# Landing tiles, residual rows and the order of W's transfers in the 16-point stage of a spectral kernel

## The chip, the cores and the metric

The kernel runs on one core of one Trainium2 chip. The metric is the device time of one execution in microseconds (us). Engines: TensorE (PE) multiplies, VectorE (DVE) and ScalarE (ACT) work element by element, GpSimd (POOL) and SyncE (SP) mostly issue transfers (DMAs). Each engine works its own instruction queue in order, and so does SP with the DMAs that it issues.

## What is computed

Four layers in turn on x of 2048 rows and 576 columns: a Fourier mixing layer A, a long-convolution layer B, and both again with the same matrices.

```python
def A(x):                     # y = Re(C (x W)), C: 2048 x 2048, W: 576 x 576
    a, b = x @ W_re.T, x @ W_im.T
    return C_re @ a - C_im @ b

def B(q, k, v, shift_k, ssm_k, ssm_D):
    kv = shift_conv4(k, shift_k) * v
    y = irfft(rfft(pad(kv)) * rfft(pad(ssm_k)))[:2048] + kv * ssm_D
    return q * y              # q: the normed rows

x = x + A(norm(x)); x = x + B(norm(x), K, V, ...)
x = x + A(norm(x)); x = x + B(norm(x), K, V, ...)
```

The convolution's result does not depend on x (only the gate q does), so it is computed once, beside the first layer A, and used by both layers B.

## The kernel before, in words

**Layer A.** C (`c_mat`) is walked in steps of one 128x512 piece: `layer` (L297) loops over four blocks of output rows (tb), two parts (g: real, imaginary) and 16 pieces (k). That is 128 steps for the first layer A, 32 to a block. A step has 14 matmuls of 512 columns: 12 into four accumulators `s`, 2 into `rm` for the last 64 columns of x (the remainder rows). `load_c` (L214) keeps two pieces in flight: it loads a piece into a raw tile (ring `craw`) by a DMA on SP, and splits it into a rounded high part (ACT, L93) and a low part (DVE, L94) in tiles `cs` (three of them, in `mats`). Each such load is kept behind the one before it, and `load_after` (L165) keeps other loads behind the newest of them. At the end of a g (steps 15, 31, 47, 63 and so on) the accumulators are split into `u`, and `evac_r` (L263) brings the remainder rows through a scratch tile (ring `rt`, words RT_AT on of the big tile `flts`): ACT copy L269, DVE add L270, then a split (ACT L93, DVE L94, written `u<-flts`).

**Hidden rows.** When a block is done, its four groups of 128 rows are multiplied by W in `hidden` (L273): a residual row x is loaded (SP, L276), and for each half of 288 columns 27 matmuls go into one PSUM tile `bk`, which DVE adds to the residual (L284); then the row is stored (`done0`, SP, L686) into `xa`. There are three `bk` tiles, shared with the convolution. Two residual tiles of 576 words (ring `res`) are in turn. At the end of the first g of the next block (steps 47, 79, 111) PE works through those of the four rows that are left.

**W.** `load_w` (L226) brings W in nine pieces through a ring of three raw tiles `wl` (DMAs on SP: L233, the last piece L235 and L236), and ACT and DVE split each (L93 and L94, from the fifth on L105 and L106). It runs from step 41 to 45.

**The convolution** is a generator, `branch` (L344), of which the main loop takes a piece now and then. Its first part (to step 42) ends in stores `t<-flts` from a ring of four tiles `so`. Its second part, the 16-point stage, begins at step 45 (`MID_LOAD`) and is spread from step 47 to 111 by planned costs. It works a list `feeds` of 96 items: 64 "mid" items (16-point transforms and the product with the kernel, 9 matmuls of 288 columns: `mid_kernel`, `mid_signal`, `mid_inverse`), whose results go to `v_d` (`vd<-flts`, ACT queue), and 32 rows of the inverse (`i2_products`, 12 matmuls), which read `v_d`. Ten of the 16 inverse rows of the first half stand between the mid items of the second half, every second one from item `I2_FIRST` on; the others come after the last mid item. Each item's input, a feed, is loaded into a landing tile (ring `land`, two of 576 words; `flts<-t` for a mid item, `flts<-vd` for an inverse row, both issued from SP at L167), then split by `act_split` (ACT L509 for the first and L507 after that, DVE L513) two items ahead of its use. After item i the feed i+4 is asked for, into the tile from which feed i+2 has just been split. All ACT work of this stage is kept in the order of the program (L504 to L509).

**The order of the work** on each engine's queue is made when the program is built: a planner goes by program order, dependences (overlapping words of a tile are one) and a model of costs, and may bring an instruction forward that has nothing to wait for. `behind(...)` and `issue_after` keep an instruction behind a named one on the same engine.

**The words of `flts`** in the 16-point stage: two raw tiles `craw` (512 words) in 88 to 1111; `res` 1112 to 2263; `land` 2264 to 3415; `kk` 3416 to 4567; four `vo` tiles of 288 from 4568 to 5719; `rt` 5464 to 5975. Before that stage `so` lay in 1112 to 3415 and the W tiles `wl` lie in 3416 to 5143.

Of the kernel before, what the change touches and what calls it, by code (L numbers as in the profile page):

```python
# [13 lines left out]
OP = mybir.AluOpType  # L14

P = 128
S = 2048
D = 576
J = S // P
TB = 4  # L20
NT = 512
HD = D // 2
NC = 4
REM = D - NC * P
# [15 lines left out]
I2_END = 111  # L40
PREP = 113
MID_LAG = 2
BORDER = {J - 1: 0.5, 0: 0.75}
I2_FIRST = 37
I2_LATE = 6
I2_COST = 2.0
GROUPS = 2
# [6 lines left out]
CRAW = 2  # L54
# [6 lines left out]
SC_AT = 8 + 4 * STAT  # L61
RT_AT = SC_AT + 4 * REM + 5 * WIDE
# [4 lines left out]
def fnet_h3_kernel(ctx: ExitStack, tc: tile.TileContext, x, c_mat, w_re, w_im, k_pad, v, shift_k,  # L67
                   ssm_k, ssm_d, f1c, i2c, midc, out):
    nc = tc.nc
# [26 lines left out]
    @contextmanager  # L96
    def behind(*instructions):
        with ExitStack() as stack:
            for i in instructions:
                stack.enter_context(tc.issue_after(i))  # L100
            yield
# [27 lines left out]
    ring = {}  # L129

    def lay(t, at, *sizes):

        for name, words, n in sizes:
            ring.setdefault(name, Ring()).tiles.extend(t[:, at + i * words:at + (i + 1) * words] for i in range(n))
            at += n * words
        assert at <= t.shape[1], (at, t.shape, sizes)
        return at
# [18 lines left out]
    flts = flat(FLT, F32, "flts")  # L156
# [6 lines left out]
    anchor, made, rounded, pows, biased, halved, added, evac, parted, stored = [], [], [], [], [], [], [], [], [], []  # L163

    def load_after(dst, src):  # L165
        with tc.issue_after(anchor[-1]):
            return nc.sync.dma_start(dst, src).ins  # L167
# [37 lines left out]
    xa_d = [dr.tile([P, D], F32, name=f"xa{j}") for j in range(J)]  # L205
# [15 lines left out]
            halved[:] = split(t[0], t[1], raw)  # L221
        CT[step] = t

    W = []

    def load_w():  # L226
        lay(flts, SC_AT + CRAW * NT + 4 * D, ("wl", D, 3))
        wg = region_a(FR, "w").rearrange("p (k n) -> p k n", k=9)
        for ch in range(9):
            w = two(wg[:, ch])  # L230
            raw = ring["wl"]()
            if ch < 8:
                nc.sync.dma_start(raw, (w_re if ch < 4 else w_im)[(ch % 4) * P:(ch % 4 + 1) * P, :])  # L233
            else:
                nc.sync.dma_start(raw[:REM], w_re[NC * P:, :])  # L235
                nc.sync.dma_start(raw[REM:], w_im[NC * P:, :])  # L236
            if ch < 4:
                split(w[:, 0, :], w[:, 1, :], raw)
            else:
                signed_split(w[:, 0, :], w[:, 1, :], raw, -1.0 if ch < 8 else mixed)  # L240
            W.append(w)
            yield
        for ch in range(9):
            load_after(w_d[ch], wg[:, ch].bitcast(F32))
            yield
# [26 lines left out]

    def hidden(us, tb, jj, xres, done, late=False):  # L273
        j = TB * tb + jj
        r = ring["res"]()
        (load_after if late else nc.sync.dma_start)(r, xres(j))  # L276
        for hf in range(2):
            ps = bank()
            cs = slice(hf * HD, (hf + 1) * HD)
            for ch in range(9):  # L280
                for n, (a, b) in enumerate(((0, 0), (0, 1), (1, 0))):
                    mm(ps[:, :HD], us[ch][:, a, jj * P:(jj + 1) * P], W[ch][:, b, cs],
                       ch == 0 and n == 0, ch == 8 and n == 2)
            added[:] = [nc.vector.tensor_tensor(r[:, cs], r[:, cs], ps[:, :HD], OP.add).ins]  # L284
            yield
        done(j, r)

    def finish(pending, pieces):
        while pending and pieces:
# [54 lines left out]
    def branch():  # L344
# [131 lines left out]
        for left_over in split_up:  # L476
            yield from f1_products(*left_over)
        m1 = region_b(FR, "mid")
        kk_at = SC_AT + CRAW * NT + 4 * D
        at = lay(m1, 0, ("df", 2 * D, 3), ("mc", 4 * P, 1))  # L480
        fresh("land", "fc")
        old = ring["craw"]
        held = [t for t in (old() for _ in range(3)) if t is not old.tiles[CRAW]]
        fresh("craw")
        ring["craw"].tiles.extend(held)
        spare = at
        at = lay(m1, at, ("yf", D, 2))
        lay(m1, at, ("fc", 4 * P, 2))
        at = lay(flts, SC_AT + CRAW * NT, ("res", D, 2))
        lay(flts, at, ("land", D, 2), ("kk", D, 2), ("vo", HD, 4))  # L490
        mc = quads(ring["mc"]())
        load_fr(mc, midc)
        lo, hi = slice(0, 64), slice(64, 128)
# [74 lines left out]
        def load_feed(i):  # L568
            if i < len(feeds):
                kind, hf, q = feeds[i]  # L570
                landed[i] = ring["land"]()
                load_after(landed[i], v_d[hf][:, q].rearrange("p c d -> p (c d)") if kind else
                           t_d[hf][4 * q:4 * q + 4].rearrange("q j c s d -> (q j c) (s d)"))
# [8 lines left out]
                halves[i] = parts("df")  # L582
                act_split(*halves[i], landed.pop(i))

        load_feed(0)
        load_feed(1)
        yield 0
        for i in range(2):
            split_feed(i)
            load_feed(i + 2)  # L590
            load_fc(i)
        used, ahead, product = 0, 2, None
        for i, (kind, hf, q) in enumerate(feeds):
            df = halves.pop(i)
            if kind:
                i2_products(hf, q, fcs.pop(used), df)
                load_fc(used + ahead)
                used += 1
            else:
                if len(yfs) == MID_LAG:  # L600
                    mid_inverse(*yfs.pop(0))
                    yield 0.4
                kk = mid_kernel(df)
                if product is not None:
                    yfs.append((*product[:2], mid_round(product[2])))
                yield 1.6
                product = hf, q, mid_signal(df, kk)
            split_feed(i + 2)
            load_feed(i + ahead + 2)
            if i == last_mid:  # L610
                yield 0.4
                mid_inverse(*yfs.pop(0))
                yfs.append((*product[:2], mid_round(product[2])))
                while yfs:
                    yield 0.4
                    mid_inverse(*yfs.pop(0))
                for name, t, at, words in (("fc", m1, spare, 4 * P), ("land", flts, kk_at, D)):
                    old = ring[name]
                    held = [old.tiles[(old.n + m) % 2] for m in range(2)]
                    fresh(name)  # L620
                    lay(t, at, (name, words, 2))
                    ring[name].tiles.extend(held)
                for m in range(2):
                    load_fc(used + ahead + m)
                    load_feed(i + ahead + 3 + m)
                ahead = 4
            yield I2_COST if kind else 1.1

# [53 lines left out]
            next(ln, 0)  # L682
            X[j] = to_x(src, j)

    def done0(j, xa):
        nc.sync.dma_start(xa_d[j], xa)  # L686

    def make_x1(j):
        xa, q = ring["xa"](), ring["yb"]()
# [63 lines left out]
    for n, whole in layer(get_x0, lambda j: x[:, j, :], done0, pending):  # L753
        if (whole or whole is not None and n % J < J - 1) and n <= F1_END:
            at = n if whole else n - 0.5
            at16 = 4 + 2 * F1_16
            want = int(4 + F1_16 * at / 8 if at <= 16 else at16 + (68 - at16) * (at - 16) / (F1_END - 16))
            with behind(made[min(n + 2, J - 1)], *evac):
                while used < want:
                    next(br)  # L760
                    used += 1
        if whole is not None and n >= W_FROM and len(W) < 9:
            with behind(*stored):
                next(wl)
        if whole and n == MID_LOAD:
            next(br)
        if n >= MID_FROM:
            if whole is not None:
                passed += STEP * (4 if whole else 3) / 7 * BORDER.get(n % J, 1.05)
            if whole is None or whole and n % 2 == 1 and n % (2 * J) < J - 1 and pending:  # L770
                finish(pending, 1)
                passed += PIECE
            near = whole and n % J == J - 2 or whole is False and n % J == J - 1
            for _ in range(0 if near else GROUPS):
                if spent < work * min(1.0, passed / total):
                    with behind(*added, *evac):
                        spent += next(br, work)
        if not whole:
            continue
        if n >= W_SAVE and n % 2 == 0:  # L780
            next(wl, 0)
        m = n - PREP
        if m == 0:
            lay(flts, SC_AT + CRAW * NT + 2 * D, ("xa", D, 2), ("yb", D, 2))
            old = ring["craw"]
            held = [old(), old()]
            fresh("craw")
            lay(flts, SC_AT + CRAW * NT + 6 * D, ("craw", NT, 1))
            ring["craw"].tiles.extend(held)
            gate = region_b(F32, "gate")  # L790
            lay(gate, 0, ("xa", D, 4), ("yb", D, 4), ("xj", D, 2))
        if 0 <= m and n < HOLD:
            advance(m // 2 if m % 2 == 0 and m < 2 * EARLY else None)
# [328 lines left out]
```

## Time and profile before

| | |
|---|---|
| runs shown | 1197.28, 1197.49, 1197.61 us; median 1197.49 |
| profiled execution | 1196.82 us, of which the span from first to last instruction is 1195.0 |
| granted clock of PE | 0.999 |
| PE busy | 1175.8 us |
| DVE, ACT, POOL busy | 839.1, 637.5, 74.0 us |
| DMA queue of SP | 205.58 MB |

How to read the profile's lines: `L76 PE MATMUL bk<-mid 128x288 ... x627 | 106.9, 299 | 2.9 <-ACT ...` is a group of instructions of line 76 that write `bk` and read `mid`: how many, busy us in total, mean ns of one, and the idle time of the engine just before them with what ended it. In a list of waits, "SPq L167 <- DVE mid L513: total, times, longest" says that the DMA issued at line 167 waited for DVE's instruction of line 513. In a timeline a row has start and duration in us; what stands in brackets is the idle time before it and who ended it. Durations of matmuls overlap, so their mean is longer than the distance from one to the next.

### The profile page before, as it was taken

Reading aid. Unit: us, or ns where it says so; the run is one execution under the profiler, and the core shown is the slowest. Engines: PE = TensorE matmul, PEld = TensorE weight load, DVE = VectorE, ACT = ScalarE, POOL = GpSimd, SP = SyncE. Lnnn points to the kernel's source line nnn. Section 1 sums busy time; section 2 is a strip of 40 time slices with the busy share of each in tenths; the row PEclk is TensorE's granted clock in tenths of the full one; section 3 lists DMA queues with packets and bytes.
Section 4 is the critical chain, followed back from the end, with each engine's and each line's share of the span. In section 5 each row is a group of like instructions: output and inputs, shape, how many; then the busy total and the mean of one; then the engine's idle time right before and its main releaser. Section 6 shows DMA issues by size and latency. Waiting matters only on the chain.

```text
span 1195.0 us, 18251 instructions
## 1 busy us (share of the span) xinstructions
PE 1175.8 (98%) x6320; PEld 1028.1 (86%) x6320; DVE 839.1 (70%) x1495; ACT 637.5 (53%) x1266; POOL 74.0 (6%) x116
## 2 busy tenths in 40 slices
PE   7999999999999999999999999999999999999997
PEld 6888888988888888889988898888888888889997
DVE  7899794679877677675447766774775776874764
ACT  7965655477766567665435666544434435540200
POOL 2200000000000000001101121000000000001111
PEclk9999999999999999999999999999999999999999
DMA  9889898546756657658967686872592597696621
GB/s 355 279 268 308 258 300 279 154 136 192 210 190 191 216 165 220 200 143 240 317 198 242 221 255 215 272 266 71 168 313 93 163 317 273 201 350 190 219 83 41
DMA packets 146110, 261.96 MB, mean 219 GB/s; under 512 B 15841, under 2 KB 44769, under 8 KB 146018
## 3 DMA queue, kind: packets, MB, share of 16 engines
q1 hardware_dynamic: 102674, 205.58, 54.1%
q10 hardware_dynamic: 36432, 42.63, 10.2%
q0 software_dynamic: 6912, 12.59, 4.0%
q8 instruction: 50, 0.82, 0.3%
q14 instruction: 42, 0.34, 0.1%
HBM read 194.09 MB, written 66.65 MB: 218 GB/s over the span
## 4 chain that ended last, share of the span: by engine, by line
PE 74%; ACT 3%; DVE 3%; issue 1%; DMA 1%; ACTq 0%; POOLq 0%; DVEq 0%
PE s L76 41%; PE bk L76 29%; PE rm L76 4%; ACT flts L507 2%; DVE mid L513 1%; ACT mid L507 1%; DMA flts<-t 1%; DVE u L94 0%; DVE flts L527 0%; DMA flts<-vd 0%; ACT u L93 0%; DVE flts L526 0%; DVE flts L528 0%; ACT mats L93 0%; DVE flts L270 0%
## 5 line engine op out<-in xcount | busy, mean ns | idle before, releaser
L76 PE MATMUL s<-mats 128*128 128x512 f32 x2088 | 528.2, 392 | 0.3 <-DVE u L94 0.2
L76 PEld LDWEIGHTS s<-mats 128*128 128x128 f32 x2088 | 381.5, 188 | 69.2 <-DVE u L94 0.6
L93 ACT ACTIVATE mats<-flts 128x512 fp32r<-128x512 f32 x201 | 125.8, 627 | 91.5 <-PE rm L76 33.4
L94 DVE TENSOR_TENSOR mats<-flts,mats 128x512 fp32r<-128x512 f32 x201 | 137.3, 687 | 51.6 <-ACT mats L93 50.4
L507 ACT ACTIVATE flts<-bk 64x288 f32<-64x288 f32 (+1 forms) x288 | 115.7, 406 | 105.0 <-PE bk L76 83.0
L513 DVE TENSOR_TENSOR mid<-flts,mid 128x576 fp32r<-128x576 f32 (+1 forms) x160 | 102.0, 638 | 45.6 <-ACT mid L507 38.0
L76 PE MATMUL bk<-mid 128*128 128x288 f32 x768 | 128.5, 298 | 2.9 <-ACT flts L507 1.8
L76 PEld LDWEIGHTS bk<-mid 128*128 128x128 f32 x768 | 114.8, 188 | 19.1 <-ACT flts L507 7.7
L76 PE MATMUL bk<-w,u 128*128 128x288 f32 x864 | 120.5, 295 | 1.5 <-DVE flts L284 1.0
L76 PEld LDWEIGHTS bk<-w,u 128*128 128x128 f32 x864 | 117.4, 188 | 4.8 <-DVE flts L284 1.7
L76 PE MATMUL rm<-mats 128*128 128x512 f32 x304 | 94.4, 390 | 0.0
L507 ACT ACTIVATE mid<-flts 128x576 fp32r<-128x576 f32 (+1 forms) x159 | 87.0, 581 | 12.0 <-DMA flts<-vd 6.7
L443 ACT ACTIVATE flts<-bk 128x288 f32<-128x288 f32 x128 | 50.7, 409 | 48.1 <-PE bk L76 47.5
L76 PEld LDWEIGHTS bk<-f1r 128*128 128x128 f32 x384 | 59.8, 192 | 13.2 <-ACT f1r L93 6.4
L76 PE MATMUL bk<-f1r 128*128 128x288 f32 x384 | 64.6, 301 | 6.7 <-ACT f1r L93 6.4
L76 PE MATMUL bk<-mats 128*128 128x288 f32 (+1 forms) x376 | 67.9, 317 | 0.0
L284 DVE TENSOR_TENSOR flts<-flts,bk 128x288 f32<-128x288 f32 x48 | 21.8, 453 | 65.0 <-PE bk L76 64.9
L76 PEld LDWEIGHTS rm<-mats 128*128 128x128 f32 x304 | 56.9, 188 | 11.8
L76 PE MATMUL s<-t,mats 128*128 128x512 f32 x264 | 64.9, 389 | 0.0
L185 POOL TENSOR_TENSOR flts<-flts 128x1 f32<-128x1 f32 x35 | 29.6, 844 | 522.7 <-DVE flts L184 522.7
L76 PE MATMUL bk<-mats,t 128*128 128x288 f32 (+1 forms) x368 | 59.3, 303 | 0.0
L76 PEld LDWEIGHTS bk<-mats 128*128 128x128 f32 x376 | 55.6, 188 | 3.4
(148 smaller groups left out, 1434.2 us busy)
## 6 DMA issues: line engine op xcount, KB each, us to landing
flts<-in_c_mat SPq DMA_DIRECT2D x148, 256.0 KB, 3.7
ph<-in_c_mat SPq DMA_DIRECT2D x54, 512.0 KB, 4.5
t<-flts ACTq DMA_DIRECT2D x64, 288.0 KB, 4.9
flts<-t SPq DMA_DIRECT2D x64, 288.0 KB, 3.1
flts<-in_c_mat SPq DMA_DIRECT2D x30, 512.0 KB, 5.1
vd<-flts ACTq DMA_DIRECT2D x64, 144.0 KB, 2.9
flts<-vd SPq DMA_DIRECT2D x32, 288.0 KB, 4.5
mid<-in_i2c POOLq DMA_DIRECT2D x32, 256.0 KB, 5.1
```

What stands on the lines that cost most here:

```text
L76: nc.tensor.matmul(ps, lhsT, rhs, start=first, stop=last, skip_group_check=more)
L93: a = nc.scalar.activation(h, src, AF.Copy).ins
L94: return a, nc.vector.tensor_tensor(l, src, h.bitcast(F32), OP.subtract).ins
L185: pows.append(nc.gpsimd.tensor_tensor(rs, ve, mhalf, OP.pow).ins)
L284: added[:] = [nc.vector.tensor_tensor(r[:, cs], r[:, cs], ps[:, :HD], OP.add).ins]
L443: stored[:] = [nc.scalar.activation(so[:, c, :], ps[:, :HD], AF.Copy).ins]
L507: last_act.append(nc.scalar.activation(*args, **kw).ins)
L513: nc.vector.tensor_tensor(l, src, h.bitcast(F32), OP.subtract)
```

## The change

Five edits, with new places for tiles:

1. `LANDS = 3`: three landing tiles (2552 to 4279); after item i the feed i+5 is asked for (later i+7 where it was i+6), and three feeds are asked for at the start.
2. `I2_FIRST` goes from 37 to 38: the first late row, and the nine that follow, stand one item later.
3. In the first layer A a residual row is loaded as two halves by two DMAs into a ring of three tiles of 288 words (1112 to 1975), and each half is stored by a DMA of its own once the next piece is taken. The late rows of the second layer stay whole.
4. The residual rows' loads, and the start of the 16-point stage, are kept behind the last DMA of W on SP.
5. Places in the stage: the two raw tiles of `c_mat` lie at 8 to 519 and at RT_AT (5464 to 5975, the place of `rt`); `vo` at 520 to 1095 and 1976 to 2551; `kk` 4280 to 5431. At step 113 three raw tiles are laid anew.

```diff
+LANDS = 3
-I2_FIRST = 37
+I2_FIRST = 38
@@ load_w
-                nc.sync.dma_start(raw[REM:], w_im[NC * P:, :])
+                asked[:] = [nc.sync.dma_start(raw[REM:], w_im[NC * P:, :]).ins]
@@ hidden
-        r = ring["res"]()
-        (load_after if late else nc.sync.dma_start)(r, xres(j))
+        if late:
+            r = ring["res"]()
+            load_after(r, xres(j))
+            rows = [r[:, :HD], r[:, HD:]]
+        else:
+            rows = [ring["res"]() for _ in range(2)]
+            with behind(*asked):
+                for hf in range(2):
+                    nc.sync.dma_start(rows[hf], xres(j)[:, hf * HD:(hf + 1) * HD])
...
-            added[:] = [nc.vector.tensor_tensor(r[:, cs], r[:, cs], ps[:, :HD], OP.add).ins]
+            added[:] = [nc.vector.tensor_tensor(rows[hf], rows[hf], ps[:, :HD], OP.add).ins]
             yield
-        done(j, r)
+            if not late:
+                done(j, cs, rows[hf])
+        if late:
+            done(j, r)
@@ branch
-        kk_at = SC_AT + CRAW * NT + 4 * D
+        kk_at = 1976 + 2 * HD + LANDS * D
...
-        old = ring["craw"]
-        held = [t for t in (old() for _ in range(3)) if t is not old.tiles[CRAW]]
         fresh("craw")
-        ring["craw"].tiles.extend(held)
...
-        at = lay(flts, SC_AT + CRAW * NT, ("res", D, 2))
-        lay(flts, at, ("land", D, 2), ("kk", D, 2), ("vo", HD, 4))
+        lay(flts, lay(flts, 8, ("craw", NT, 1)), ("vo", HD, 2))
+        lay(flts, RT_AT, ("craw", NT, 1))
+        at = lay(flts, SC_AT + CRAW * NT, ("res", HD, 3), ("vo", HD, 2), ("land", D, LANDS))
+        assert at == kk_at
+        assert lay(flts, at, ("kk", D, 2)) <= RT_AT
...
-        load_feed(0)
-        load_feed(1)
+        for i in range(LANDS):
+            load_feed(i)
         yield 0
         for i in range(2):
             split_feed(i)
-            load_feed(i + 2)
+            load_feed(i + LANDS)
             load_fc(i)
...
             split_feed(i + 2)
-            load_feed(i + ahead + 2)
+            load_feed(i + ahead + LANDS)
...
-                    held = [old.tiles[(old.n + m) % 2] for m in range(2)]
+                    held = [old.tiles[(old.n + m) % len(old.tiles)] for m in range(len(old.tiles))]
...
-                    load_feed(i + ahead + 3 + m)
+                    load_feed(i + ahead + LANDS + 1 + m)
@@ done0
-    def done0(j, xa):
-        nc.sync.dma_start(xa_d[j], xa)
+    def done0(j, cs, xa):
+        nc.sync.dma_start(xa_d[j][:, cs], xa)
@@ main loop of the first layer
         if whole and n == MID_LOAD:
-            next(br)
+            with behind(*asked):
+                next(br)
...
         if m == 0:
...
-            old = ring["craw"]
-            held = [old(), old()]
             fresh("craw")
             lay(flts, SC_AT + CRAW * NT + 6 * D, ("craw", NT, 1))
-            ring["craw"].tiles.extend(held)
+            lay(flts, SC_AT, ("craw", NT, CRAW))
```

More of the change, by code (lines that the diff above doesn't have):

```diff
@@ L222, in load_c @@
         CT[step] = t
-    W = []
+    W, asked = [], []
     def load_w():
```

## The prediction

> **What bounds the kernel now.** I read the head of the page first, then busy time by stretches, then the groups of TensorE (PE) instructions in the stretch that the change touches, then the waits, and last the chain of waits.
>
> ```profile
> span 1195.0 us, 18251 instructions
> PE 1175.8 (98%) x6320; PEld 1028.1 (86%) x6320; DVE 839.1 (70%) x1495; ACT 637.5 (53%) x1266; POOL 74.0 (6%) x116
> ```
>
> PE is the bound, and the change removes no matmul. All that it can win is time in which PE is held up, and only between about 200 us (W arrives) and 550 us (the last 16-point item). A row of busy time by stretches has for each engine the busy us and the instructions in brackets.
>
> ```profile
> 200.00:550.00 350.00, 345.35 (x1960) 303.25 (x1959) 261.02 (x503) 229.33 (x493) 6.50 (x13) 1.00 0.62 187
> 200.00:225.00 25.00, 23.72 (x136) 20.67 (x135) 13.96 (x24) 12.12 (x23) 1.21 (x3) 1.00 0.74 222
> 440.00:460.00 20.00, 18.83 (x101) 15.39 (x100) 18.28 (x36) 16.10 (x36) 1.05 (x2) 1.00 0.69 201
> 1076.00:1176.00 100.00, 100.00 (x757) 100.00 (x756) 61.27 (x130) 11.58 (x18) 14.10 (x14) 1.00 0.45 148
> ```
>
> PE is idle 350 - 345.35 = 4.65 us there. Matmuls overlap, so idle time understates the loss; the pace is the better measure. Undisturbed pace of 512-column matmuls, from the timeline of PE (start, us, what): 12 + 2 of them between 625.81 and 628.99, 3.18 / 14 = 0.227 us each. Of 288-column ones, which alone run at the end: 100 / 757 = 0.132 us.
>
> ```profile
> 625.81 2.88 PE L76 MATMUL s<-mats 128*128 128x512 f32 x12
> 628.53 0.62 PE L76 MATMUL rm<-mats 128*128 128x512 f32 x2
> 628.99 2.88 PE L76 MATMUL s<-mats 128*128 128x512 f32 x12
> ```
>
> The groups of PE in 200 to 550:
>
> ```profile
> L76 PE MATMUL s<-mats 128*128 128x512 f32 x706 | 183.3, 392 | 0.2 <-DVE u L94 0.2
> L76 PE MATMUL bk<-mid 128*128 128x288 f32 x627 | 106.9, 299 | 2.9 <-ACT flts L507 1.8 <-DVE flts L527 0.3
> L76 PE MATMUL bk<-w,u 128*128 128x288 f32 x509 | 71.3, 296 | 1.5 <-DVE flts L284 1.0 <-DVE w L106 0.3 <-ACT flts L507 0.2
> L76 PE MATMUL rm<-mats 128*128 128x512 f32 x118 | 36.5, 390 | 0.0
> ```
>
> 824 x 0.227 + 1136 x 0.132 = 187.0 + 150.0 = 337.0 us; 350 - 337.0 = **13 us is all there is to win**, 1.1% of the kernel. The Trainium skill (Perfetto Trace Analysis, Identifying the Most-Contended Engine) would judge the headroom by the busy share of weight loads; here that is 303.25 of 350, which would leave 47 us, but the same share is 86% over the whole kernel, where most stretches lose nothing, so the pace decides.
>
> **The change part by part.** *(a) W ahead of the residual rows.* SyncE (SP) works its queue in order. Four of its rows, from its timeline:
>
> ```profile
> 201.95 0.33 SPq L276 DMA_DIRECT2D flts<-in_x  x1
> 204.24 0.33 SPq L167 DMA_DIRECT2D flts<-t  x1
> 204.69 0.42 SPq L233 DMA_DIRECT2D flts<-in_w_im  x1
> 208.67 0.34 SPq L167 DMA_DIRECT2D flts<-t  x1
> ```
>
> A residual row (201.95) and the first feed of the 16-point stage (204.24) stand ahead of a W piece (204.69), which so goes at least 204.69 - 201.95 = 2.7 us later than SP came to the first of them. PE pays when the first hidden row reaches the last W pieces (waits of PE in 205 to 225: total, times, longest):
>
> ```profile
> PE bk L76 <- DVE flts L284: 1.0, 2, 0.7
> PE bk L76 <- DVE w L106: 0.3, 1, 0.3
> ```
>
> The 0.3 is W's own split; the 1.0 is the add of the first half row, late because VectorE (DVE) works W's and c_mat's splits ahead of it. Earlier W pieces clear both: -1.3, bounds 0 and -1.3. Against it stands the first feed: the new landing tiles (words 2552 to 4279) lie on the last two store tiles of the stage before and on W's raw tiles, so the first feed can no longer go at 204.24 but about where the second goes now, 208.67. The second's split on ScalarE (ACT) was
>
> ```profile
> 215.15 0.67 ACT L507 ACTIVATE mid<-flts 128x576 fp32r<-128x576 f32 x1
> 216.00 0.43 PE L76 MATMUL bk<-mid 128*128 128x288 f32 x2
> ```
>
> and PE's first 16-point matmul began at 216.00. A first feed that is split at 215.15 is ready at 215.82 on ACT and some 0.7 later on DVE: +0 to +0.6. I take +0.3. Sum of (a): **-1.0**, bounds -1.3 and +0.6.
>
> *(b) Third landing tile.* With two tiles, feed i+4 goes where feed i+2 lay; with three, feed i+5 does. Both wait for the same split, at the same place in the program: SP's wait stays, but the data has one item more before it is needed. The place where that matters is 440 to 460, where late rows (feeds from vd) lie between the 16-point feeds (from t). The chain of waits there, and ACT at its end:
>
> ```profile
> 442.42 2.85 DMA flts<-vd
> 451.97 3.49 DMA flts<-t
> 454.74 0.68 ACT L507 ACTIVATE mid<-flts 128x576 fp32r<-128x576 f32 x1 [1.36 <-DMA flts<-vd]
> ```
>
> 6.3 of these 20 us of the chain are transfers into landing tiles. PE's groups in 440 to 460:
>
> ```profile
> L76 PE MATMUL s<-mats 128*128 128x512 f32 x42 | 12.4, 393 | 0.0
> L76 PE MATMUL bk<-mid 128*128 128x288 f32 x51 | 9.7, 304 | 1.2 <-ACT flts L507 1.0
> L76 PE MATMUL rm<-mats 128*128 128x512 f32 x8 | 2.5, 393 | 0.0
> ```
>
> 50 x 0.227 + 51 x 0.132 = 18.1 of 20 us: **1.9 us lost**. I take all of it as won: the late DMA comes first in that chain. If ACT (16.10 busy of 20) and DVE (18.28) are late next, it is 0. The other bound is all the time that ACT waits for feeds in 200 to 550:
>
> ```profile
> ACT mid L507 <- DMA flts<-vd: 4.4, 5, 1.4
> ACT mid L507 <- DMA flts<-t: 1.7, 2, 1.3
> ```
>
> 4.4 + 1.7 = 6.1. So (b): **-1.9**, bounds -6.1 and 0. The late rows one item later (I2_FIRST) cancel the longer lead for these rows: the first late feed is asked for after the same item as before, so it waits no longer for the store of the half that it reads. Cost 0. After the last 16-point item the lead is seven feeds, not six; PE waits for nothing from 550 to 630 beyond what (b) covers. Cost 0.
>
> *(c) Residual rows in halves.* 16 rows of one load and one store become 32 of each, so 32 more issues of 0.33 us on SP, 11 us in some 400 in which SP mostly waits. What counts is what SP waits for at them (waits of SP in 224 to 630):
>
> ```profile
> SPq L167 <- DVE mid L513: 175.6, 86, 5.5
> SPq L276 <- DMA xa<-flts: 25.2, 10, 5.2
> SPq L686 <- DVE flts L284: 18.6, 10, 5.3
> ```
>
> A load of a row waits for the store of an older row to land (2.5 us), a store for its add (1.9 us); behind them stand feeds and c_mat loads. Halves double these waits and shift the stores forward by half a row. While SP waits there, the feed behind it would mostly wait for its split (2.0 us each) anyway: cost 0; without that cover, as much as (b) wins, +1.9, since it is the feeds that come late. The Trainium skill (DMA: Bandwidth & Descriptors, Rules for kernel authors) speaks against this part: many small transfers are to be put together, since a fixed part dominates. The trace agrees on the fixed part:
>
> ```profile
> flts<-t SPq DMA_DIRECT2D x64, 288.0 KB, 3.1
> vd<-flts ACTq DMA_DIRECT2D x64, 144.0 KB, 2.9
> ```
>
> Half the bytes take 2.9 instead of 3.1 us to land, so two halves in a row would take 2.7 us more for each row. This falls on PE only if something waits for it; a half row is needed some 3.5 us after its matmuls begin (27 x 0.132), as now.
>
> *(d) c_mat's raw tiles.* One of the two now lies where the remainder rows' scratch tile (rt) lies. At each block end (steps 47, 63, 79, 95, 111) the load of c_mat four steps on has to wait until that tile's last reader, DVE's split, is done, where it now goes ahead. Step 79 from the timelines of SP, DVE and ACT, and the issue row of c_mat:
>
> ```profile
> 428.60 0.33 SPq L167 DMA_DIRECT2D flts<-in_c_mat  x1
> 440.08 0.69 DVE L94 TENSOR_TENSOR u<-flts,u 64x512 fp32r<-64x512 f32 x1
> 441.82 0.63 ACT L93 ACTIVATE mats<-flts 128x512 fp32r<-128x512 f32 x1
> flts<-in_c_mat SPq DMA_DIRECT2D x148, 256.0 KB, 3.7
> ```
>
> The load moves from 428.60 to 440.77, lands at 440.8 + 3.7 = 444.5, and its split, now at 441.82, moves 2.7 us back. PE needs that matrix only at step 83, three steps after the end of step 79; 50 matmuls of 512 in 20 us are 3.6 steps of 14, so a step takes 5.6 us here and 16 us remain. The shortest time is after step 111, where a step takes 3.18 us and step 115 begins at 628.99 (above):
>
> ```profile
> 621.84 0.68 DVE L94 TENSOR_TENSOR u<-flts,u 64x512 fp32r<-64x512 f32 x1
> ```
>
> 622.5 + 3.7 + 1.3 for the split = 627.5, 1.5 us to spare. So cost 0 if ACT does other work meanwhile; up to +2.7 at each of the four ends inside the stage if ACT stands at that split with 16-point work queued behind it: +10.8.
>
> **Sum:** -1.0 - 1.9 + 0 + 0 = -2.9 us on the profiled execution (1196.82 us: the span of 1195.0 and 1.8 around it). The median of the runs shown is 1197.49, 0.7 above it; the forecast is 1197.5 - 2.9 = **1194.6 us**, by itself 1192.5 to 1196. About 0.2% (2.4 us) is what a measurement of this kernel tells from no change, so the forecast lies close to that edge.
>
> **The rivals.**
>
> *Hidden, or taken back.* PE's stalls between 250 and 440 come from ACT and DVE in turn, not from transfers (of PE's idle time before 16-point matmuls, 1.8 of 2.9 us ends with ACT's copy L507). Where the feed comes earlier, the same chain is late next; or the half rows delay the feeds on SP by as much as the third tile gives them. For it: DVE's 18.28 of 20 us. Against it: ACT does wait for the feed at 454.74. Then only (a) is left, or less: 1197.5 - 0.5 = **1197.0**.
>
> *More freedom.* The feed one item earlier lets ACT and DVE run ahead throughout: all 6.1 us of (b) and 1.0 of (a): **1190.4**. Against it: the order of ACT's 16-point work is fixed by the program.
>
> *c_mat stands in ACT's way (slower).* As in (d): ACT works in order and waits at the block ends for a c_mat that came late. It decides once more than 2.9 us reach PE, so from the second block end on. Three of four ends: 3 x 2.7 = 8.1, less 2.9 won: +5.2, **1202.7**. For it: the exact tiles that collide, and the tight stretch behind step 79. Against it: the order is made knowing the dependence, and four steps of slack.
>
> *The change doesn't do what it says.* If the first feed is as late as in (a)'s worst case and W no earlier, (a) is +0.6 and (b) still holds: 1196.2, inside the first two cases.
>
> **How the numbers follow.** Forecast 0.44, hidden 0.30, more freedom 0.07, slower 0.19. Faster by over 0.2%: 0.8 of the forecast (0.35), all of more freedom (0.07) and a little of hidden: 0.44. Within 0.2%: the rest of the forecast (0.09), most of hidden (0.24) and a little of the slower case: 0.35. Slower: 0.21. Range 1190.8 to 1203.0: it leaves out the far ends of the second and third rival, about 0.2.
>
> **What would show it.** (a): W's issues on SP without an L276 between them, and no PE wait on L106 in 205 to 225. (b): ACT's waits for feeds (4.4 and 1.7 us) below 2, and PE's loss by pace in the stretch of the first late rows below 1 us. (c): SP's waits for xa and L284 grow, with no c_mat or feed wait on ACT. (d): the c_mat loads after steps 63, 79, 95 issued behind the remainder rows' split; ACT waiting for c_mat there would be the slower rival. Wrong would be the whole account if PE's loss by pace in 200 to 550 stays at 13 us and the time moves all the same.

## The result and the profile after

The changed kernel takes **1193.97 us** (median of 12 runs, 1192.70 to 1196.82), the one before, run beside it, 1197.40 (1195.87 to 1198.31). The ratio is **0.9974, 95% interval 0.9967 to 0.9982**: 3.4 us or 0.3% faster, where 2.9 were forecast (1194.6). The profiled execution of the changed kernel took 1196.82 us and is the slowest of its twelve, so its stretches are of use and its total isn't. Its head, from the page (lines of the code have moved by 1 to 11: L77 is L76 of before, L518 L507, L524 L513, L292 L284, L284 L276, L697 L686, L168 L167, L520 L509):

```profile
span 1195.0 us, 18305 instructions
PE 1176.4 (98%) x6320; PEld 1026.8 (86%) x6320; DVE 839.1 (70%) x1495; ACT 637.3 (53%) x1266; POOL 74.2 (6%) x116
```

54 instructions more, none of them work of PE, DVE or ACT: 32 are the half rows' DMAs, and 22 more, on balance, are waits for semaphores. Busy time in the stretches of the prediction:

```profile
200.00:550.00 350.00, 347.37 (x1979) 306.02 (x1978) 261.92 (x505) 229.83 (x495) 6.11 (x12) 1.00 0.63 189
200.00:225.00 25.00, 24.46 (x147) 21.87 (x146) 15.18 (x26) 11.48 (x21) 0.29 (x1) 1.00 0.73 230
440.00:460.00 20.00, 19.91 (x111) 17.13 (x110) 18.96 (x38) 16.89 (x38) 1.58 (x3) 1.00 0.85 247
```

Where 101 matmuls ran between 440 and 460 us there are now 111; between 200 and 225, 147 instead of 136. PE's groups in 200 to 550:

```profile
L77 PE MATMUL s<-mats 128*128 128x512 f32 x708 | 183.9, 392 | 0.1
L77 PE MATMUL bk<-mid 128*128 128x288 f32 x640 | 108.8, 298 | 2.0 <-ACT flts L518 1.0 <-DVE flts L538 0.3
L77 PE MATMUL bk<-w,u 128*128 128x288 f32 x513 | 71.6, 295 | 0.5 <-DVE flts L292 0.5
L77 PE MATMUL rm<-mats 128*128 128x512 f32 x118 | 36.8, 390 | 0.0
```

At the pace of the prediction 826 x 0.227 + 1153 x 0.132 = 339.7 us of work stand in these 350, so **10.3 us are lost where 13.0 were**. Of what is left, 6.1 us lie between 250 and 440 us, where 6.5 were lost before: the change hardly reaches that stretch. Idle time ended by W's split (L106 before, L107 now) is gone, the add's is halved.

What stands in the profiled execution and not in others is late. PE's waits after 600 us:

```profile
PE s L77 <- ACT ph L867: 1.5, 1, 1.5
PE s L77 <- DVE u L95: 0.3, 1, 0.3
```

In the chain of waits ahead of the first of them, 14 us earlier, stands one slow transfer of `c_mat`:

```profile
735.96 6.21 DMA flts<-in_c_mat
```

### The profile page after: what moved, and what is told of

Read it like the earlier page. It is cut to its first block, busy times and chain, and to the rows that moved or that the text cites. A ratio compares the mean times of both kernels' runs of the same rounds, so it can differ in the third digit from the quotient of the medians.

```text
span 1195.0 us, 18305 instructions
## 1 busy us (share of the span) xinstructions
PE 1176.4 (98%) x6320; PEld 1026.8 (86%) x6320; DVE 839.1 (70%) x1495; ACT 637.3 (53%) x1266; POOL 74.2 (6%) x116
## 3 DMA queue, kind: packets, MB, share of 16 engines
q10 hardware_dynamic: 36432, 42.63, 10.3%
## 4 chain that ended last, share of the span: by engine, by line
PE 69%; DVE 5%; ACT 3%; DMA 2%; issue 2%; POOL 0%; ACTq 0%; SPq 0%; DVEq 0%; POOLq 0%
PE s L77 38%; PE bk L77 29%; PE rm L77 3%; DVE mid L524 1%; ACT flts L518 1%; DMA flts<-in_c_mat 1%; DVE mats L95 1%; DVE flts L538 1%; ACT mats L94 1%; DMA mid<-in_i2c 0%; DVE flts L537 0%; ACT mid L518 0%; DVE u L95 0%; DMA ph<-in_c_mat 0%; DMA gate<-xa 0%
## 5 line engine op out<-in xcount | busy, mean ns | idle before, releaser
L77 PE MATMUL s<-mats 128*128 128x512 f32 x2088 | 528.6, 392 | 2.0 <-ACT ph L867 1.5
L77 PEld LDWEIGHTS s<-mats 128*128 128x128 f32 x2088 | 380.7, 188 | 72.8 <-ACT ph L867 2.4
L518 ACT ACTIVATE flts<-bk 64x288 f32<-64x288 f32 (+1 forms) x288 | 116.0, 407 | 109.9 <-PE bk L77 93.1
L524 DVE TENSOR_TENSOR mid<-flts,mid 128x576 fp32r<-128x576 f32 (+1 forms) x160 | 102.0, 638 | 47.5 <-ACT mid L518 41.4
L77 PE MATMUL bk<-mid 128*128 128x288 f32 x768 | 128.6, 298 | 2.3 <-ACT flts L518 1.0
L77 PEld LDWEIGHTS bk<-mid 128*128 128x128 f32 x768 | 114.9, 188 | 18.0 <-ACT flts L518 5.8
L77 PE MATMUL bk<-w,u 128*128 128x288 f32 x864 | 120.2, 295 | 0.5 <-DVE flts L292 0.5
L77 PEld LDWEIGHTS bk<-w,u 128*128 128x128 f32 x864 | 117.4, 188 | 3.5 <-DVE flts L292 1.2
L77 PE MATMUL rm<-mats 128*128 128x512 f32 x304 | 94.7, 390 | 0.0
L518 ACT ACTIVATE mid<-flts 128x576 fp32r<-128x576 f32 (+1 forms) x159 | 87.0, 583 | 6.3 <-DVE flts L539 2.2
L77 PE MATMUL bk<-f1r 128*128 128x288 f32 x384 | 64.4, 300 | 6.5 <-ACT f1r L94 6.3
L77 PEld LDWEIGHTS bk<-f1r 128*128 128x128 f32 x384 | 59.4, 191 | 13.0 <-ACT f1r L94 6.6
L77 PE MATMUL bk<-mats 128*128 128x288 f32 (+1 forms) x376 | 67.8, 317 | 0.0
L77 PEld LDWEIGHTS rm<-mats 128*128 128x128 f32 x304 | 56.9, 188 | 12.1 <-ACT flts L518 0.2
L292 DVE TENSOR_TENSOR flts<-flts,bk 128x288 f32<-128x288 f32 x48 | 21.8, 453 | 63.6 <-PE bk L77 63.3
L77 PE MATMUL s<-t,mats 128*128 128x512 f32 x264 | 65.2, 389 | 0.0
L77 PE MATMUL bk<-mats,t 128*128 128x288 f32 (+1 forms) x368 | 59.3, 303 | 0.0
L77 PEld LDWEIGHTS s<-t,mats 128*128 128x128 f32 x264 | 49.5, 188 | 10.7 <-DVE mats L200 0.4
```

The lines of the kernel that those rows point to most:

```text
L77: nc.tensor.matmul(ps, lhsT, rhs, start=first, stop=last, skip_group_check=more)
L292: added[:] = [nc.vector.tensor_tensor(rows[hf], rows[hf], ps[:, :HD], OP.add).ins]
L518: last_act.append(nc.scalar.activation(*args, **kw).ins)
L524: nc.vector.tensor_tensor(l, src, h.bitcast(F32), OP.subtract)
```

## The experiments

Each kernel was run beside the one before, in four groups of runs (its medians: 1197.40 to 1197.44 us). The ratios carry the verdicts; the medians are for orientation. The changed kernel itself ran in the first two groups only (the first two rows of the table), so the kernels from the sixth row on are compared with it through their ratios. A loss "by pace" is the prediction's measure: the length of a stretch, less 0.227 us for each 512-column and 0.132 us for each 288-column matmul in it. Each such loss comes from one profiled execution, and the changed kernel's two differ by up to 0.4 us in a stretch.

| kernel | median us | ratio to before, 95% interval |
|---|---|---|
| changed | 1193.97 | 0.9974 (0.9967 to 0.9982) |
| changed, once more | 1194.22 | 0.9969 (0.9958 to 0.9981) |
| before + W first | 1195.53 | 0.9984 (0.9975 to 0.9993) |
| changed, two landing tiles | 1198.63 | 1.0006 (0.9996 to 1.0015) |
| changed, rt on vo | 1194.76 | 0.9974 (0.9963 to 0.9984) |
| before + half rows | 1198.38 | 1.0012 (1.0002 to 1.0022) |
| two landing tiles, rt on vo | 1197.39 | 1.0008 (0.9999 to 1.0016) |
| before + W first + third tile | 1196.12 | 0.9988 (0.9979 to 0.9997) |
| changed, lead of six feeds | 1194.38 | 0.9976 (0.9967 to 0.9985) |
| changed, whole rows | 1194.82 | 0.9975 (0.9965 to 0.9984) |
| changed, W not first | 1194.89 | 0.9984 (0.9974 to 0.9993) |

**The changed kernel again**, no edit.

> The changed kernel once more, as the mark for the other runs. Its profiled execution above took 1196.82 us where the median was 1193.97, with a PE stall at 749.8 us behind a c_mat transfer of 6.2 us. Theory (the gain lies in 200 to 550 us, that late stall is an accident of one execution): ratio to the kernel before 0.9974 again, within 0.0010; PE's loss by pace in 200 to 550 about 10 us, no stall of over 1 us at 750. Rival (the change pushes the later stages' transfers): the stall near 750 is there again.

Measured: 1194.22 us, ratio 0.9969, and 9.9 us lost by pace between 200 and 550. No wait of PE after 600 us at all: the stall at 749.8 us was an accident of one execution. The rival falls.

**W first alone**, on the kernel before:

```diff
-        (load_after if late else nc.sync.dma_start)(r, xres(j))
+        with behind(*(() if late else asked)):
+            (load_after if late else nc.sync.dma_start)(r, xres(j))
...
         if whole and n == MID_LOAD:
-            next(br)
+            with behind(*asked):
+                next(br)
```

> The kernel before with only W's transfers ahead of the residual rows and of the stage's first feeds. Theory: part (a) alone, 1.0 us less than before (0.3 to 1.5), ratio 0.9992; PE's waits for L106 and L284 in 205 to 225 (1.3 us before) below 0.6; the stretch 440 to 460 still loses 1.9 us. Rival (the third tile does all, or the reshuffled order does): within 0.3 us of before.

Measured: -1.9 us (1197.44 to 1195.53); the ratio's interval is 0.8 to 3.0 us less, so the forecast's term of 1.0 lies inside it. Its stretches:

```profile
440.00:460.00 20.00, 18.92 (x102) 15.59 (x102) 18.14 (x35) 16.15 (x37) 1.05 (x2) 1.00 0.75 222
200.00:225.00 25.00, 25.00 (x148) 22.39 (x147) 15.16 (x26) 12.54 (x24) 1.46 (x3) 1.00 0.78 237
```

148 matmuls instead of 136 between 200 and 225 and no idle time; between 440 and 460 nothing has changed (102, before 101). So the two gains have two places, and this one is W's.

**Two landing tiles**, on the changed kernel:

```diff
-LANDS = 3
+LANDS = 2
-I2_FIRST = 38
+I2_FIRST = 37
```

> The changed kernel with two landing tiles and the first late row at 37, all else as changed. Theory: part (b) is gone, 1.9 us more than the changed kernel (1 to 3), so ratio to before about 0.9990; ACT's waits for feeds in 224 to 550 back above 3 us, PE's loss in 440 to 460 back to some 2 us. Rival (half rows, new places or order bring the gain, the tile is hidden): within 0.5 us of the changed kernel.

The late rows' place goes back together with the tile. Measured: 1198.63 us, 4.4 more than the changed kernel beside it (1194.22), and no longer faster than before, though W is first. Its stretch of the first late rows, and the two longest of PE's waits after 200 us:

```profile
440.00:460.00 20.00, 17.86 (x95) 14.58 (x95) 17.23 (x34) 14.28 (x33) 1.05 (x2) 1.00 0.72 216
```

```profile
PE bk L77 <- ACT flts L518: 3.5, 9, 1.2
PE bk L77 <- DMA mid<-in_i2c: 1.6, 1, 1.6
```

95 matmuls: fewer than before the change (101). By pace 3.3 us are lost here (44 matmuls of 512 columns, 51 of 288), 0.4 in the changed kernel. Another 1.7 us are lost between 550 and 575 (0.6 and 0.4 in the changed kernel's two executions), where PE waits for a load of `in_i2c`; these loads are issued from POOL, and why this one is late isn't shown. The two stretches hold most of the 4.4 us. The first late feed, in its chain of waits:

```profile
441.04 4.40 DMA flts<-vd
```

It takes 4.40 us where 2.85 were on the path before. So the third tile is worth more than the 1.9 us read from the trace of before: it also pays for what the other edits cost. Three kernels of this group give the steps: W first alone 1195.53; with half rows and new places, on two tiles, 1198.63, so 3.1 more (2.6 by ratios); with the third tile 1194.22, so 4.4 less.

**The scratch tile rt off `c_mat`'s raw tile**, on the changed kernel:

```diff
         lay(flts, RT_AT, ("craw", NT, 1))
+        fresh("rt")
+        lay(flts, 520, ("rt", NT, 1))
...
-            fresh("craw")
+            fresh("craw", "rt")
+            lay(flts, RT_AT, ("rt", NT, 1))
```

> The changed kernel with the remainder rows' scratch tile moved, in the stage, off c_mat's raw tile onto the words of two vo tiles. In the changed kernel's trace SP waits 23.8 us at five block ends for the remainder rows' split ahead of a c_mat load, and ACT waits 11.5 us for c_mat in 224 to 640. Theory (part d costs nothing: four steps of slack): those waits go, the time stays within 0.6 us of the changed kernel. Rival (d eats a part of the gain): 1 to 2.5 us less than the changed kernel.

Measured: 1194.76 us, 0.5 more than the changed kernel beside it; the intervals cover each other. ACT's waits for `c_mat` in 224 to 550 were 5.2 us in the changed kernel (below) and are now

```profile
ACT mats L94 <- DMA flts<-in_c_mat: 0.2, 1, 0.2
```

The collision is real, its wait is gone, and the time doesn't follow: the rival's 1 to 2.5 us aren't there. ACT waits for no store out of a `vo` tile in that kernel either, so no price of the new place shows that could hide a gain.

**Half rows alone**, on the kernel before, in the words of the two whole tiles:

```diff
-        r = ring["res"]()
-        (load_after if late else nc.sync.dma_start)(r, xres(j))
+            rows = [ring["res"]() for _ in range(2)]
+            for hf in range(2):
+                nc.sync.dma_start(rows[hf], xres(j)[:, hf * HD:(hf + 1) * HD])
...
-        at = lay(flts, SC_AT + CRAW * NT, ("res", D, 2))
+        at = lay(flts, SC_AT + CRAW * NT, ("res", HD, 4))
```

> The kernel before with only the residual rows in halves: two loads and two stores for each of the 16 rows, four half tiles in the words of the two whole ones. Theory (part c costs nothing by itself, SP's longer waits fall where it would wait for a split anyway): within 0.5 us of before; SP's waits for xa and for L284's add up from 25 and 19 us to 32 and 38 as in the changed kernel. Rival (half rows delay the feeds, so that the third tile only repairs what they break): 1.5 to 3 us more than before, ACT's waits for feeds in 224 to 550 above 6 us.

Measured: ratio 1.0012, so 0.2 to 2.6 us more; the median is 0.9 more. The theory of no cost falls. SP's waits in 224 to 630 did grow, those for the adds by less than it says (28.8, not 38):

```profile
SPq L282 <- DMA xa<-flts: 32.2, 18, 4.0
SPq L695 <- DVE flts L290: 28.8, 21, 2.5
```

43.8 us before, 61.0 now; its wait for the feeds' splits fell meanwhile from 175.6 to 157.6 us. By pace the loss sits in two places: 200 to 225 us (2.7, before 1.6) and 550 to 575 (1.1, before none). The first shows in the waits of PE, and in DVE's timeline in front of the longest.

```profile
PE bk L76 <- DVE flts L290: 2.4, 2, 1.8
```

```profile
223.08 0.76 DVE L522 TENSOR_TENSOR mid<-flts,mid 128x576 fp32r<-128x576 f32 x1 [2.03 <-ACT mid L516]
223.76 0.45 DVE L290 TENSOR_TENSOR flts<-flts,bk 128x288 f32<-128x288 f32 x1
```

DVE stands 2.03 us at the split of a feed, and behind it in its queue stands the add that frees the PSUM tile for which PE waits. The chain of waits there has the feed's transfer:

```profile
217.68 4.66 DMA flts<-t
```

In the kernel before, the same feed took 3.12 us and went at 218.25. So at this place the feed isn't asked for late; its transfer is longer. A half row's store goes just ahead of it (217.01), but that it slows the feed isn't shown. The rival's delayed feeds are therefore only partly right: ACT's waits for feeds in 224 to 550 didn't rise above 6 us, and this one, at 220, lies outside that window.

**Two landing tiles and rt on vo**: both edits above together.

> The kernel with two landing tiles (4.4 us more than the changed kernel, 1.2 more than the one before) with the remainder rows' scratch tile moved onto two vo tiles, so that no c_mat load waits for it. Theory (the c_mat load held back to the block end collides with the feed behind it, 4.4 us to land where it was 2.9; with a third tile that is covered, with two it is paid): 1 to 2.5 us less than with two tiles, PE's loss in the stretch of the first late rows down by 1 us. Rival (the half rows make it): within 0.5 us of the kernel with two tiles.

Measured: 1197.39, by medians 1.2 less than with two tiles; by ratios (1.0008 and 1.0006) nothing. Between 440 and 460 us

```profile
440.00:460.00 20.00, 18.91 (x102) 15.67 (x101) 17.68 (x35) 15.62 (x36) 1.05 (x2) 1.00 0.79 216
```

102 matmuls instead of 95, 1.9 us lost by pace instead of 3.3: there the held-back `c_mat` load does cost what the theory says. Whether the whole time follows stays open.

**W first and the third tile with whole rows**, on the kernel before; two `vo` tiles make the room:

```diff
-        lay(flts, at, ("land", D, 2), ("kk", D, 2), ("vo", HD, 4))
+        lay(flts, at, ("land", D, LANDS), ("kk", D, 2), ("vo", HD, 2))
```

> The kernel before with W first, three landing tiles and the first late row at 38, but whole residual rows and c_mat's raw tiles where they were; two vo tiles instead of four make the room. Theory (W first and the third tile are the whole gain, half rows and new places only make room): ratio 0.997 like the changed kernel's, within 0.8 us of it. Rival (two vo tiles are too few: the copies out of PSUM wait for their stores): no better than W first alone, with waits of ACT for vd or yb transfers.

Measured: 1196.12, ratio 0.9988: no better than W first alone. But both sides are half right. Between 200 and 550 us this kernel loses 9.1 us by pace, the least of all, so there the theory holds: W first and the third tile are the gain, without half rows. Much of it is given back between 550 and 630, where 2.7 us are lost (0.2 before, 0.8 and 0.9 in the changed kernel). ACT's waits for stores, in 224 to 550 and in 550 to 630:

```profile
ACT flts L509 <- DMA vd<-flts: 1.6, 2, 1.4
```

```profile
ACT flts L509 <- DMA yb<-flts: 14.2, 7, 3.0
```

ACT's copies out of PSUM wait for the stores of the two tiles, as the rival says, above all in the last inverse rows (`yb`); in the kernel before and in the changed one ACT waits for none of these stores in 224 to 640 us. The third tile needs its 576 words, and two vo tiles are too dear a place to take them from.

**A lead of six feeds after the last 16-point item**, on the changed kernel:

```diff
-            load_feed(i + ahead + LANDS)
+            load_feed(i + ahead + lead)
...
-                    load_feed(i + ahead + LANDS + 1 + m)
-                ahead = 4
+                    if not m:
+                        load_feed(i + ahead + LANDS + 1)
+                ahead, lead = 4, 2
```

> The changed kernel with the lead after the last 16-point item at six feeds, as before the change, instead of seven. In the changed kernel SP stands from 551 to 556 us for a vd store that the first feed of the second half reads, and holds a c_mat load and feeds behind it; PE loses some 0.5 us there that it did not lose before. Theory: 0.5 us less than the changed kernel (0 to 1), SP's wait for vd moves behind the c_mat load. Rival (that loss has another cause): no change in that stretch.

Measured: 1194.38 us, the same, and SP's wait for the store between 545 and 570 us is what it was (4.8 us in both):

```profile
SPq L168 <- DMA vd<-flts: 4.8, 2, 2.8
```

The lead isn't what puts SP there, and the kernel before waited 5.1 us for such a store in the same stretch. The chain of waits of the changed kernel's first profiled execution reaches PE at 556.6 us by another way, a load of `in_i2c` that POOL issues:

```profile
550.84 5.65 DMA mid<-in_i2c
```

In its second execution, and in this kernel, the chain there has PE's own work alone. So by these chains SP's wait isn't what reaches PE near 556 us; what makes the small loss in the other executions stays open.

**Whole rows**, on the changed kernel, with three vo tiles:

```diff
-        at = lay(flts, SC_AT + CRAW * NT, ("res", HD, 3), ("vo", HD, 2), ("land", D, LANDS))
+        at = lay(flts, SC_AT + CRAW * NT, ("res", D, 2), ("vo", HD, 1), ("land", D, LANDS))
```

> The changed kernel with whole residual rows (two tiles of 576 words, one load and one store a row) in place of halves; one of the four vo tiles makes the room. Theory (half rows cost about 1 us by themselves, as in the kernel before with halves alone, and three vo tiles are enough): 0.5 to 1.2 us less than the changed kernel, about 1193.3, with the late rows' stretch unchanged. Rival (the third tile covers the half rows' delays, or three vo tiles make ACT's copies wait for stores): the same as the changed kernel, or up to 1 us more, with waits of ACT for vd transfers.

Measured: 1194.82, ratio 0.9975, the changed kernel's. The theory isn't borne out: whole rows win nothing that can be measured. That fits the rival in both its forms, and they aren't parted: the third tile may cover the half rows' delays, or the missing vo tile may eat the gain (ACT waits 1.8 us for a `yb` store in 224 to 640 us, never in the changed kernel). A little is lost at the first hidden rows (waits of PE in 205 to 225: 0.9 us, 0.5 in the changed kernel):

```profile
PE bk L77 <- DVE flts L287: 0.9, 2, 0.7
```

**W not first**, on the changed kernel: the two `behind(*asked)` taken away.

> The changed kernel with the residual rows and the stage's start no longer kept behind W's last transfer. Theory (a): 1.5 to 2 us more than the changed kernel, lost in 205 to 225 where the first hidden row waits for W's last pieces, as W first alone took 1.9 us off the kernel before. Rival (the landing tiles lie on W's raw tiles, so two of the three feeds come after W in any case): 0 to 0.7 us more.

Measured: 1194.89, ratio 0.9984: 0.7 to 0.9 us more by medians, 1.2 to 1.8 by ratios to the two measurements of the changed kernel. The interval (0.9974 to 0.9993) doesn't part theory from rival. PE's waits in 205 to 225 (0.5 and 0.2 us in the changed kernel's two executions):

```profile
PE bk L77 <- DVE flts L291: 0.8, 2, 0.6
```

**The late row at item 37 beside three tiles** (`I2_FIRST = 37`, expected within 0.5 us of the changed kernel) has no time to compare: its feed is asked for after item 33, ahead of the store, made at item 34, that it reads, so it loads words that nothing has written yet. So with the longer lead the move to 38 is needed, and what it is worth by itself can't be read from these runs.

## Why the prediction was right, step by step

**(a) W first: right, its terms a little too small.** Forecast -1.0, alone -1.9 (0.8 to 3.0). The sign named for it is there: no residual row stands between W's issues, and PE waits for no split of W. Two terms were mis-sized. The -1.3 was PE's idle time; by pace, as in the prediction's first part, 200 to 225 lost 25 - 57 x 0.227 - 79 x 0.132 = 1.6 us, and in the kernel with W first alone nothing is lost there. (In the changed kernel 0.7 and 0.2 us are still lost there, behind the adds of half rows.) And the +0.3 for the late first feed can't be seen. The last DMA of W before the change:

```profile
207.06 0.57 SPq L236 DMA_DIRECT2D flts<-in_w_im  x1
```

The start of the stage in the changed kernel's second execution, on SP, ACT and PE:

```profile
204.75 0.57 SPq L237 DMA_DIRECT2D flts<-in_w_im  x1
205.36 0.63 SPq L236 DMA_DIRECT2D flts<-in_w_re  x1
209.37 0.82 SPq L168 DMA_DIRECT2D flts<-t  x2
```

```profile
210.15 0.78 ACT L106 ACTIVATE w<-flts 128x576 fp32r<-128x576 f32 x1 [0.74 <-DMA flts<-in_w_re]
212.83 0.69 ACT L520 ACTIVATE mid<-flts 128x576 fp32r<-128x576 f32 x1 [1.38 <-DMA flts<-t]
```

```profile
216.00 0.44 PE L77 MATMUL bk<-mid 128*128 128x288 f32 x2
```

The first feed goes at 209.37, as (a) said, five us later than before, but is split at 212.83, not at the 215.15 that I took from the second feed of before, and PE comes to it at 216.00 as ever. It is ready 2.3 us earlier than the sum took it to be.

**(b) The third tile: right as read, more than read.** The 1.9 us lost between 440 and 460 became 20 - 52 x 0.227 - 59 x 0.132 = 0.4:

```profile
L77 PE MATMUL s<-mats 128*128 128x512 f32 x44 | 12.4, 393 | 0.0
L77 PE MATMUL bk<-mid 128*128 128x288 f32 x59 | 10.2, 299 | 0.1
L77 PE MATMUL rm<-mats 128*128 128x512 f32 x8 | 2.6, 392 | 0.0
```

ACT's waits for transfers in 200 to 550 (W's aside) are now

```profile
ACT mats L94 <- DMA flts<-in_c_mat: 5.2, 4, 2.2
ACT mid L520 <- DMA flts<-t: 1.5, 1, 1.5
ACT mid L518 <- DMA flts<-t: 0.7, 1, 0.7
```

The 4.4 us for feeds from vd are gone; the 1.5 is the stage's first feed, 3.9 before, which the prediction's 6.1 left out. Neither ACT nor DVE was late next there (PE's idle time is 0.1 us): the rival "hidden, or taken back" falls in that stretch. Without the tile the changed kernel is 4.4 us slower, not 1.9. In that stretch 1.4 us of the difference go when rt moves off `c_mat`'s tile, so part of the rest is the price of (d), which the tile covers. How the remainder divides among half rows, the new places and the late `in_i2c` load isn't shown. The late rows' move (I2_FIRST) is, by the program, what the longer lead asks for.

**(c) Half rows: cost 0 fits beside the third tile, its reason only in part.** The reason was that "the feed behind it would mostly wait for its split anyway". Half rows alone cost about 1 us (0.2 to 2.6), with two tiles, so there the cover isn't whole. In the changed kernel whole rows are no faster, which fits cost 0, though the missing vo tile could hide a gain. That the third tile is the cover is the likeliest reading; no run shows it free of other edits. In SP's waits (224 to 630) of the changed kernel the growth is plain, twice as much for stores that wait for their add, a quarter more for loads that wait for a store:

```profile
SPq L168 <- DVE mid L524: 148.0, 84, 3.7
SPq L697 <- DVE flts L292: 37.7, 20, 7.8
SPq L284 <- DMA xa<-flts: 31.7, 16, 3.9
SPq L168 <- DVE u L95: 23.8, 5, 5.7
```

25.2 + 18.6 = 43.8 us became 69.4, while the wait for splits fell from 175.6 to 148.0: SP waits about as long, for other things, and that much of the reason holds. The rule that I weighed there (the Trainium skill, DMA: Bandwidth & Descriptors, Rules for kernel authors: put small transfers together) calls transfers under 64 KB mostly overhead. A half row is 144 KB; the 1 us that half rows alone cost points the rule's way, and the changed kernel doesn't show it. The prediction compared a load with a store of another queue. Like with like, the issues of the kernel before and of the changed one are:

```profile
flts<-in_x SPq DMA_DIRECT2D x16, 288.0 KB, 3.4
xa<-flts SPq DMA_DIRECT2D x16, 288.0 KB, 2.3
```

```profile
flts<-in_x SPq DMA_DIRECT2D x32, 144.0 KB, 2.5
xa<-flts SPq DMA_DIRECT2D x32, 144.0 KB, 2.6
```

A whole row's load lands after 3.4 us, its store after 2.3; a half row's after 2.5 and 2.6, and after 2.9 and 1.9 in the second execution. So half the bytes take clearly more than half the time.

**(d) `c_mat` in rt's words: right.** The last of the SP rows above is it, five waits at five block ends, 23.8 us, and ACT does wait 5.2 us for `c_mat`, the sign that the prediction had set for the slower rival. But PE waits for no piece of `c_mat` there, and moving rt away ends ACT's wait and not a microsecond of the time, so four steps of slack are enough. That rival, 0.19, named this mechanism rightly and its price wrongly; it shows only with two landing tiles, between 440 and 460.

**The sum**, -2.9, lies inside the measured interval (2.2 to 4.0 us less), so the 0.5 us to the median needs no cause. Part of the closeness is luck. In this order of the edits, from W first alone to the changed kernel, (c), (d) and the new places cost 3.1 us by medians and the third tile wins 4.4, together -1.3. The prediction had 0 and -1.9: both terms were too small, and the errors mostly cancel.

## What to carry to other kernels

Where PE is the bound, count what it loses by pace and not by idle time, stretch by stretch: here that gave both places of the gain, and the size of the one where it was used for the sum. A buffer more in a ring that feeds a queue worked in order can be worth more than the wait that it removes (4.4 us here, 1.9 read), for it can also cover what else is put on that queue; so test each edit on the kernel that will have it, and not alone. Look behind the stretch that an edit is for, too: with two vo tiles instead of four the third landing tile won its time up to 550 us, and much of that was lost after. Where a load moves to a later time, ask how long its data would have lain there before it was used.

## What the runs showed of the hardware that was not expected

Each of the twelve executions profiled here has at least five loads of `c_mat` (256 KB), and up to eleven, that took over 6 us from issue to landing, where the medians are 3.6 to 3.9. One of them, of 6.2 us, was followed by a stall of PE of 1.5 us, nearly half of what the change wins: by the chain of waits it held up ACT, and behind ACT a store of `y` and the next load of `ph`. No other execution shows PE waiting over 1 us after 600 us. So the slow load by itself is common; why this one found no slack isn't shown.

Single executions of one kernel lie up to 6.5 us apart (half rows alone, 1196.81 to 1203.30; the changed kernel's first twelve 4.1). The profiled execution took 1196.82 us both before the change and after it, so for a change of 0.3% its own total says nothing.
